# Block-sparse attention scores: four heads at a time in row tiles, with the chunk mask added by 32-row matmuls

## The chip, the cores and the metric

The kernel runs on one core of a Trainium2 chip. The metric is device microseconds for one execution. The kernel before takes 304.92 us (median of three runs, 304.57 to 305.27). Engines are named as in the profile: PE is TensorE (matmuls), PEld its weight loads, DVE VectorE, ACT ScalarE, POOL GpSimd, SP SyncE.

## What is computed

Attention in which each query looks at six chunks of 32 keys, followed by a gated feed-forward layer. Batch 4, 8 heads, 768 positions, head width 64; the feed-forward is 512 to 1536 to 512 on 3072 tokens. The reference, cut:

```python
chunk, top_k, scale = 32, 6, 1 / sqrt(64)
k_min, k_max = k_chunks.min(axis=3), k_chunks.max(axis=3)
ub = sum(maximum(q * k_min, q * k_max), axis=-1)        # a bound for each query and chunk
ub = where(causal, ub, -1e9)
top_chunks = argsort(ub)[..., -top_k:]
scores = scale * (q @ k.T)
mask = (key's chunk is in top_chunks) & (query >= key)
attn = softmax(where(mask, scores, -1e9))
x = (attn @ v)  ->  [3072, 512]
out = (sigmoid(x @ w_gate) * (x @ w_val)) @ w_out
```

## The kernel before

**Order.** The kernel is written as operations with the buffers that they read and write, the engines that may do each, an estimated cost and a rank. `Plan` walks them in estimated time and fixes for every engine one order and for every buffer one slot; the chip then runs each engine's instructions in that order, with semaphores where one engine reads what another wrote. The slots are few: eight PSUM banks (`ps`), of which at most 4 for the feed-forward (`ff`), 3 for scores (`sc`), 2 for attention output (`pv`), 3 for transposes (`pr`), 2 for the bounds (`ub`); 4 buffers `att` for exponentials.

**Tiling.** The 24 blocks of 128 queries are split into eight units of three blocks. Unit 0 holds the first blocks of three batches, which see only their own keys (`first`, scores at L661). Units 1 to 7 go through four stages. `prepare` turns keys and queries (`keys_wide`, `queries_wide` for units 1 and 2, `keys_blocks`, `turn_queries`, `queries_blocks` for the rest) and calls `choose`, which computes the bounds (L811), the sixth largest of each query (L834), and the marks of what is not chosen, turned so that a chunk is a partition (`apt`, L845). `attend` makes scores, exponentials and output; `finish` divides by the sum and turns the result into `xT`; `ffn` does the gate, value and output products (L955, L977). The rank puts `attend` of unit i beside `ffn` of unit i-1, so TensorE has both to do.

**Scores.** The two halves of the heads, `e` and `o`, use 64 partitions each of the turned tensors: head h is pair p = h mod 4, half e = h div 4. A score matmul has 128 rows. Half of them are the 64 components of a head; the other half are the mask. For that, `hk` (keys) holds in its other 64 partitions a fixed pattern `epat`, with -60000 where a partition's chunk is the key's chunk, and `hq` (queries) holds there the marks from `apt`. One matmul thus gives score plus mask. The price is that every head half has an `hk` and an `hq` of its own, filled by copies of 64 partitions (`hk0_`, `hk1_`, `hq0_`, `hq1_`, and `hqm` for the marks), which ACT, DVE or POOL does at L383, L385, L387.

`pack` cuts what a unit's queries see into pieces (key block, first query block, number of query blocks) and lays them into banks of 512 columns. Over units 1 to 7 there are 55 pieces for each head in 23 banks. `attend` goes head by head and bank by bank: one operation `sc` of two to four matmuls into one PSUM bank (L872), one exponential of the bank on ACT (L883), a causal cut of the first bank on POOL (L889), and a head later the output matmuls `pv` (L905). After two heads comes `finish`.

The score matmul:

```python
nc.tensor.matmul(at(t)[:, o:o + 128 * m], hk[b % 2][e_][:, p, 128 * jb:128 * jb + 128],
                 hq[u.side][e_][:, p, 128 * x:128 * (x + m)], start=True, stop=True)
```

Of the kernel before, what the change touches and what calls it, by code (L numbers as in the profile page):

```python
# [15 lines left out]
NEG = -60000.0  # L16
# [322 lines left out]
def kernel(  # L339
# [28 lines left out]
        {"ps": 8, "big": 2, "v": 6, "np": 7, "qf": 2, "qm": 1, "kx": 2, "kt": 3, "ubn": 1, "mx": 1, "apt": 1,  # L368
         "att": 4, "rz": 2, "x": 3, "xt": 2, "gate": 4, "hg": 18, "osb": 2},
        {("ps", "ff"): 4, ("ps", "sc"): 3, ("ps", "pv"): 2, ("ps", "pr"): 3, ("ps", "ub"): 2},  # L370
# [24 lines left out]
    hk = [[lone(f"hk{'eo'[e]}{i}", [128, NP, S]) for e in range(2)] for i in range(2)]  # L395
    hq = [[lone(f"hq{'eo'[e]}{i}", [128, NP, T]) for e in range(2)] for i in range(2)]
# [6 lines left out]
    MASK = [slice(64, 128), slice(0, 64)]  # L403
# [85 lines left out]
    epat = Buf("att", "epat", [64, 2, NC, CH], F16)  # L489
    const("ident", {POOL: (560, 600)}, lambda e: make_identity(nc, ident32), writes=["ident32"], prio=-20)  # L490
    const("epat0", {DVE: (480, 560)}, lambda e: nc.vector.memset(at(epat), 0.0), writes=[epat], prio=-3)

    def pattern(e):
        for i in range(2):
            t = at(epat)[32 * i:32 * i + 32, i]
            nc.gpsimd.affine_select(out=t, in_=t, compare_op=ALU.not_equal, fill=NEG, base=0,
                                    pattern=[[-1, NC], [0, CH]], channel_multiplier=1)

    const("epat", {POOL: (2000, 2040)}, pattern, reads=[epat], writes=[epat], prio=-2.4)
# [3 lines left out]
    for e_ in range(2):  # L503
        const(f"hq{e_}", {DVE: (150, 160)}, lambda e, e_=e_: nc.vector.memset(hq[1][e_][MASK[e_], :, 0:64], 0.0),
              writes=[("hqm", 1, e_, p, "zero") for p in range(NP)])
    for i in range(2):
        const(f"ap{i}", {DVE: (400, 410)}, lambda e, i=i: nc.vector.memset(ap[i], 0.0),
              writes=[("ap", i, 0), ("ap", i, 1)], prio=-0.5 + i)
        const(f"v1{i}", {POOL: (260, 300)}, lambda e, i=i: nc.gpsimd.memset(v16[i][:, :, :, D:D + 1], 1.0),
              writes=[("v16", i, jb) for jb in range(NBLK)], prio=-9 + 6 * i)  # L510
        for e_ in range(2):
            for o in range(2):
                const(f"hkp{i}{e_}{o}", {DVE: dve(2 * S, 4, 64), POOL: pool(2 * S), ACT: act(2 * S, False, 64)},
                      lambda e, i=i, e_=e_, o=o: copy(e, hk[i][e_][MASK[e_], o::2], at(epat)[:, o].rearrange(
                          "p c s -> p (c s)").unsqueeze(1).to_broadcast([64, NP // 2, S])),
                      reads=[epat], writes=[("hkp", i, e_, p) for p in range(o, NP, 2)], prio=0.3 + 0.2 * i, port=True)
# [97 lines left out]
    def first(u, b, x, raw, base):  # L614
# [3 lines left out]
        half = {}  # L618
        for n in "kq":
            t = ps(f"{n}fT_{b}", "pr", [128, NP, 128])  # L620

            def turn(e, t=t, n=n):
                for p in range(NP):
# [3 lines left out]
            half[n] = Buf("np", f"{n}f16_{b}", [128, NP, 128], F16)  # L627
            plan.add(f"{n}f16_{b}", {ACT: act(512), DVE: dve(512)}, lambda e, t=t, h=half[n]: copy(e, at(h), at(t)),
                     reads=[t], writes=[half[n]], prio=next_())
            if n == "k" and b == 0:  # L630
# [8 lines left out]
                for e_ in range(2):  # L639
                    plan.add(f"hkf{e_}", {POOL: pool(512), DVE: dve(512, 4, 64), ACT: act(512, False, 64)},  # L640
                             lambda e, e_=e_: copy(e, hk[0][e_][ROWS[e_], :, 0:128], at(half["k"])[ROWS[e_]]),
                             reads=[half["k"]], writes=[("hk", 0, 0, e_, p) for p in range(NP)], port=True, prio=kn())
# [15 lines left out]
        def scores(e):  # L658
            for p in range(NP):
                for e_ in range(2):  # L660
                    nc.tensor.matmul(at(sc[e_])[:, p], at(half["k"])[ROWS[e_], p], at(half["q"])[ROWS[e_], p], start=True, stop=True)  # L661

        op = plan.add(f"scf_{b}", pe(8 * 56), scores, reads=[half["k"], half["q"]], writes=sc, prio=next_())
# [51 lines left out]
    def keys_wide(u, next_):  # L715
# [5 lines left out]
        for p in range(NP):  # L721
            t = turned(u, 0, p, next_)
            extremes(b % 2, u.name, p, lambda t=t: at(t).rearrange("p (c s) -> p c s", s=CH), u.t, [t], kx,
                     chunks, blocks, False, next_)
            kt = Buf("kt", f"kt_{u.name}_{p}", [128, u.t], F16)
            plan.add(f"kt_{u.name}_{p}", {ACT: act(u.t), DVE: dve(u.t)}, lambda e, t=t, kt=kt: copy(e, at(kt), at(t)),
                     reads=[t], writes=[kt], prio=next_())
            for e_ in range(2):
                plan.add(f"hk{e_}_{u.name}_{p}", {DVE: dve(u.t, 4, 64), POOL: pool(u.t), ACT: act(u.t, False, 64)},
                         lambda e, kt=kt, p=p, e_=e_: copy(e, hk[b % 2][e_][ROWS[e_], p, rows], at(kt)[ROWS[e_]]),  # L730
                         reads=[kt], writes=[("hk", b % 2, jb, e_, p) for jb in blocks], port=True, prio=next_() + 0.3)
        ranges(b % 2, u.name, kx, chunks, blocks, next_)

    def queries_wide(u, next_):
# [3 lines left out]
        for p in range(NP):  # L738
# [6 lines left out]
            for e_ in range(2):  # L745
                plan.add(f"hq{e_}_{u.name}_{p}", {ACT: act(u.t, False, 64), DVE: dve(u.t, 2, 64), POOL: pool(u.t)},
                         lambda e, p=p, e_=e_: copy(e, hq[u.side][e_][ROWS[e_], p, 0:u.t], at(u.qf)[ROWS[e_], p, 0:u.t]),
                         reads=[(u.qf, p)], writes=[("hq", u.side, e_, p)], port=True, prio=next_() + 0.3)


    def keys_blocks(b, raw, next_):
# [4 lines left out]
        for p in range(NP):  # L756
            extremes(par, f"{b}", p, lambda p=p: at(raw)[:, p], S, every, kx, slice(0, NC), blocks, True, next_)
            k16 = Buf("np", f"k16_{b}_{p}", [128, NC, CH], F16)
            kt = Buf("np", f"kt_{b}_{p}", [128, S], F16)
            plan.add(f"k16_{b}_{p}", {POOL: pool(S), DVE: dve(S, 2), ACT: act(S, False)},  # L760
                     lambda e, p=p, k16=k16: copy(e, at(k16), at(raw)[:, p]), reads=every, writes=[k16], prio=next_())
            plan.add(f"kt_{b}_{p}", {DVE: dve(S)}, lambda e, k16=k16, kt=kt: nc.vector.transpose(  # L762
                at(kt), at(k16).rearrange("p c d -> p (c d)")), reads=[k16], writes=[kt], prio=next_())
            for e_ in range(2):
                plan.add(f"hk{e_}_{b}_{p}", {POOL: pool(S), DVE: dve(S, 4, 64), ACT: act(S, False, 64)},
                         lambda e, p=p, e_=e_, kt=kt: copy(e, hk[par][e_][ROWS[e_], p], at(kt)[ROWS[e_]]),
                         reads=[kt], writes=[("hk", par, jb, e_, p) for jb in blocks], port=True, prio=next_())
# [14 lines left out]
    def queries_blocks(u, next_):  # L782
# [5 lines left out]
        for p in range(0, NP, 2):  # L788
# [3 lines left out]
            for e_ in range(2):  # L792
                plan.add(f"hq{e_}_{u.name}_{p}", {DVE: dve(2 * T, 2, 64), ACT: act(2 * T, False, 64), POOL: pool(2 * T)},
                         lambda e, p=p, e_=e_: copy(e, hq[u.side][e_][ROWS[e_], p:p + 2], at(u.qf)[ROWS[e_], p:p + 2]),
                         reads=turned_(p), writes=[("hq", u.side, e_, p + i) for i in range(2)],
                         port=True, prio=next_() + 0.1)


    def choose(u, next_):
# [6 lines left out]
        def bounds(e):  # L806
            for par, lo, hi, _ in spans:
                for m, src in enumerate((u.qf, u.qm)):
                    for p in range(NP):
                        for e_ in range(2):  # L810
                            nc.tensor.matmul(at(ub[e_])[32 * p:32 * p + 32, lo - u.s0:hi - u.s0], kcr[par][ROWS[e_], p, m, :],  # L811
# [31 lines left out]
        apt = Buf("apt", f"apt_{u.name}", [128, 2, u.n], F16)  # L843
        for e_ in range(2):
# [3 lines left out]
            for p in range(0, NP, 2):  # L848
                plan.add(f"hqm{e_}_{u.name}_{p}", {POOL: pool(2 * u.n), DVE: dve(2 * u.n, 4, 64), ACT: act(2 * u.n, False, 64)},
                         lambda e, p=p, e_=e_: copy(  # L850
                             e, hq[u.side][e_][MASK[e_], p:p + 2, u.s0:u.t],
                             at(apt)[32 * p:32 * p + 64, e_, :].unsqueeze(1).to_broadcast([64, 2, u.n])),
                         reads=[(apt, e_)], writes=[("hqm", u.side, e_, p + i) for i in range(2)], port=True, prio=next_())


    def attend(u, base):
        nb = len(u.banks)
        next_ = rank(base, 1.0, H * (3 * nb + 4) + 12)
        late = []
        for h in range(H):  # L860
            pr, last = h // 2, h % 2
            p, e_ = h % NP, h // NP
            att = Buf("att", f"att_{u.name}_{h}", [128, 1920], F16)
            b0 = 0
            for y in range(nb):
                n = 128 * sum(w[3] for w in u.banks[y])
                t = ps(f"sc_{u.name}_{h}_{y}", "sc", [128, n])

                def scores(e, t=t, y=y, p=p, e_=e_):
                    o = 0  # L870
                    for b, jb, x, m in u.banks[y]:
                        nc.tensor.matmul(at(t)[:, o:o + 128 * m], hk[b % 2][e_][:, p, 128 * jb:128 * jb + 128],  # L872
                                         hq[u.side][e_][:, p, 128 * x:128 * (x + m)], start=True, stop=True)
                        o += 128 * m

                reads = [("hk", b % 2, jb, e_, p) for b, jb, _, _ in u.banks[y]]
                reads += [("hkp", b % 2, e_, p) for b, _, _, _ in u.banks[y]] + [("hq", u.side, e_, p), ("hqm", u.side, e_, p)]
                if u.s0:
# [238 lines left out]
```

## Time and profile before

| what | value |
|---|---|
| median of three runs | 304.92 us |
| profiled execution, its own time | 305.61 us |
| span of its profile | 303.7 us |
| mean granted TensorE clock | 0.989 (0.66 between 20 and 30 us, 1.00 in the other windows of 10 us) |
| gate and value matmuls (L955) | 768 of 384 columns |
| output projection matmuls (L977) | 288 of 512 columns |
| score matmuls (L872) | 440, in 184 operations |
| attention output matmuls (L905) | 640 of 65 columns |
| exponentials of scores on ACT (L883) | 184, 90.3 us busy |
| causal cuts on POOL (L889) | 56, 28.3 us busy |

A group line reads: line, engine, operation, output and inputs by the program's names, shape, count, then busy us and mean ns of one, then the idle time of the engine just before these instructions and what ended it. For a matmul, "64\*128" is the rows and columns of the array that it uses. The end of a matmul is modelled and includes a pipeline tail, so a mean for one is longer than the step from it to the next; steps are read from starts. In a timeline a line merges instructions of one kind; its first two numbers are start and length in us. A line of waits has the total us, the number of times and the longest.

### The profile page before, as it was taken

How to read it: one execution, taken by the hardware profiler on the slowest of the kernel's cores; microseconds unless marked ns; L12 is line 12 of the kernel's file. 1: busy time of each engine (PE TensorE's matmuls, PEld its weight loads, DVE VectorE, ACT ScalarE, POOL GpSimd, SP SyncE). 2: the span in 40 equal slices, each digit the busy share in tenths (PEclk: the TensorE clock that was granted, in tenths of full speed). 3: DMA queues.
4: the chain of work that ended last, by engine and by line, in shares of the span. 5: the costliest groups of instructions: out<-in, count | busy, mean ns of one | idle time of the engine just before them, and what ended most of it. 6: DMA issues, size and time to landing. Idle time of an engine off the chain costs nothing.

```text
span 303.7 us, 6957 instructions
## 1 busy us (share of the span) xinstructions
PE 281.5 (93%) x2656; PEld 177.1 (58%) x2656; DVE 184.5 (61%) x550; ACT 203.9 (67%) x412; POOL 97.2 (32%) x158
## 2 busy tenths in 40 slices
PE   3867998999799899999999989999999999999994
PEld 2644665667456456645677555654776467755651
DVE  7684865977998499995435986855634033322420
ACT  7494685969977785956587998454785478833321
POOL 7681023815481433901022649400111011100000
PEclk9996999999999999999999999999999999999999
DMA  7999999999999959909800456101000100001002
GB/s 159 247 223 203 196 199 263 160 185 162 216 168 134 186 106 211 130 21 158 140 2 2 107 121 152 24 0 71 36 2 3 69 37 0 2 33 73 0 4 102
DMA packets 123233, 32.69 MB, mean 108 GB/s; under 512 B 111424, under 2 KB 120128, under 8 KB 123200
## 3 DMA queue, kind: packets, MB, share of 16 engines
q1 hardware_dynamic: 118448, 27.53, 50.4%
q0 software_dynamic: 4752, 4.72, 9.2%
q8 instruction: 21, 0.34, 0.5%
q14 instruction: 12, 0.10, 0.1%
HBM read 30.67 MB, written 6.29 MB: 122 GB/s over the span
## 4 chain that ended last, share of the span: by engine, by line
PE 63%; DMA 14%; DVE 11%; POOL 3%; ACT 3%; issue 2%; SPq 2%; DVEq 0%; ACTq 0%
PE o_u L977 17%; PE g_u L955 15%; PE v_u L955 15%; DMA wo<-in_moe_w_out_dram 9%; PE sc_u L872 6%; PE pv_u L905 4%; DMA vf<-in_v_dram 3%; DVE kt L762 2%; DMA k<-in_k_dram 2%; DVE kx L596 2%; PE ube_u L811 2%; DVE kcr L596 2%; SPq L551 1%; ACT att_u L883 1%; PE xps_u L932 1%
## 5 line engine op out<-in xcount | busy, mean ns | idle before, releaser
L967 DVE SCALAR_TENSOR_TENSOR hg_u<-gate_u,v_u 128x384 f16<-128x384 f16 x96 | 51.9, 547 | 81.2 <-PE v_u L955 65.1
L883 ACT ACTIVATE att_u<-sc_u 128x512 f16<-128x512 f32 (+2 forms) x184 | 90.3, 556 | 5.0 <-PE sc_u L872 4.4
L955 PE MATMUL g_u<-xT_u,wg 128*128 128x384 f16 x384 | 79.2, 329 | 1.5 <-DMA wg<-in_moe_w_gate_dram 1.5
L955 PE MATMUL v_u<-xT_u,wv 128*128 128x384 f16 x384 | 78.8, 328 | 2.0 <-DMA wv<-in_moe_w_val_dram 1.9
L963 ACT ACTIVATE gate_u<-g_u 128x384 f16<-128x384 f32 x96 | 47.2, 492 | 33.2 <-PE g_u L955 18.8
L889 POOL TENSOR_SCALAR_AFFINE_SELECT att_u<-att_u 128x384 f16<-128x384 f16 (+1 forms) x56 | 28.3, 506 | 125.3 <-ACT att_u L883 125.2
L977 PE MATMUL o_u<-wo,hg_u 128*128 128x512 f16 x288 | 66.2, 379 | 1.2 <-DMA wo<-in_moe_w_out_dram 0.9
L955 PEld LDWEIGHTS <-wg 128*128 128x128 f16 x384 | 35.8, 98 | 23.6 <-issue 1.9
L955 PEld LDWEIGHTS <-wv 128*128 128x128 f16 x384 | 36.2, 98 | 22.3 <-DMA wv<-in_moe_w_val_dram 2.3
L977 PEld LDWEIGHTS <-hg_u 128*128 128x128 f16 x288 | 27.4, 98 | 31.9 <-issue 2.2
L986 ACT ACTIVATE osb_u<-o_u 128x512 f32<-128x512 f32 x24 | 14.3, 596 | 34.0 <-PE o_u L977 28.5
L905 PE MATMUL pv_u<-v,att_u 128*128 128x65 f16 x640 | 29.8, 194 | 2.1 <-ACT att_u L883 2.0
L905 PEld LDWEIGHTS <-att_u 128*128 128x128 f16 x640 | 26.5, 98 | 8.9 <-ACT att_u L883 3.7
L872 PE MATMUL sc_u<-hqo,hko 128*128 128x128 f16 (+2 forms) x220 | 28.4, 243 | 2.4 <-ACT att_u L883 2.2
L872 PE MATMUL sc_u<-hqe,hke 128*128 128x128 f16 (+2 forms) x220 | 25.6, 243 | 0.0
L872 PEld LDWEIGHTS <-hko 128*128 128x128 f16 x220 | 16.5, 98 | 7.5 <-issue 3.4
L872 PEld LDWEIGHTS <-hke 128*128 128x128 f16 x220 | 16.3, 98 | 5.5
L588 POOL CAST v<-v 128x512 f16<-128x512 f32 x23 | 14.7, 654 | 8.7 <-DMA v<-in_v_dram 8.6
L924 DVE TENSOR_TENSOR x_u<-pv_u,rz_u 128x384 f16<-128x384 f32 (+1 forms) x28 | 14.8, 530 | 0.6
L383 ACT COPY xT_u<-xps_u 128x384 f16<-128x384 f16 (+1 forms) x19 | 9.1, 476 | 7.9 <-PE xps_u L932 7.5
L612 POOL TENSOR_SCALAR qm_u<-qf_u 128x768 f32<-128x768 f32 (+2 forms) x7 | 12.1, 1729 | 1.9 <-issue 1.8
L834 DVE MAX8 mx_u<-ubn_u 128x8 f32<-128x8 f32 (+16 forms) x152 | 12.3, 158 | 0.1
(118 smaller groups left out, 311.5 us busy)
## 6 DMA issues: line engine op xcount, KB each, us to landing
out_dram<-osb_u SPq DMA_DIRECT2D x24, 256.0 KB, 2.3
v<-in_v_dram SPq DMA_DIRECT2D x23, 256.0 KB, 4.9
k<-in_k_dram SPq DMA_DIRECT2D x12, 384.0 KB, 7.7
q<-in_q_dram SPq DMA_DIRECT2D x12, 384.0 KB, 5.3
wg<-in_moe_w_gate_dram POOLq DMA_DIRECT2D x3, 512.0 KB, 11.3
wv<-in_moe_w_val_dram POOLq DMA_DIRECT2D x3, 512.0 KB, 13.9
wo<-in_moe_w_out_dram POOLq DMA_DIRECT2D x3, 512.0 KB, 24.4
kf<-in_k_dram SPq DMA_DIRECT2D x8, 128.0 KB, 3.6
```

The costliest lines, as they stand in the source:

```text
L588: plan.add(f"v16_{b}_{ib}", {POOL: pool(H * D)}, lambda e: nc.gpsimd.tensor_copy(v16[b % 2][:, ib, :, 0:D], at(t)), reads=[t], writes=[("v ...
L834: nc.vector.max(at(mx)[:, e_, j, :], at(ubn)[:, e_, j, 0:max(8, u.seen[j])])
L872: nc.tensor.matmul(at(t)[:, o:o + 128 * m], hk[b % 2][e_][:, p, 128 * jb:128 * jb + 128], hq[u.side][e_][:, p, 128 * x:128 * (x + m)], sta ...
L883: plan.add(f"exp_{u.name}_{h}_{y}", {ACT: act(n)}, lambda e, t=t, att=att, b0=b0, n=n: nc.scalar.activation(at(att)[:, b0:b0 + n], at(t), ...
L889: nc.gpsimd.affine_select(out=dv, in_=dv, compare_op=ALU.is_ge, fill=0.0, base=0, pattern=[[0, u.m], [1, 128]], channel_multiplier=-1)
L905: nc.tensor.matmul(at(pv)[:, last, x, :], at(att)[:, c:c + 128], v16[b % 2][:, jb, h, :], start=(jb == 0), stop=(jb == ib))
L924: plan.add(f"x_{u.name}_{p}", {DVE: dve(u.t)}, lambda e: nc.vector.tensor_tensor(at(x_).rearrange("p a (e d) -> p e a d", e=2), at(pv)[:, ...
L955: nc.tensor.matmul(at(t), w16[:, c, 128 * fb:128 * fb + 128], at(u.xt)[:, c, :], start=(c == 0), stop=(c == 3))
L963: plan.add(f"tanh_{u.name}_{fb}", {ACT: act(T)}, lambda e, g=g, gate=gate: nc.scalar.activation(at(gate), at(g), AF.Tanh, scale=0.5), read ...
L967: plan.add(f"hg_{u.name}_{fb}", {DVE: dve(T)}, lambda e, w_=w_, gate=gate, hg=hg: nc.vector.scalar_tensor_tensor(at(hg), at(gate), 1.0, at ...
L977: nc.tensor.matmul(at(o), at(hgs[fc])[:, 128 * tb:128 * tb + 128], wo16[:, fc, :], start=(fc == 0), stop=(fc == NFB - 1))
L986: nc.scalar.activation(at(osb), at(o), AF.Copy, scale=0.5) if e == ACT
```

## The change

The head halves no longer have keys and queries of their own. `hk` and `hq` hold both halves, 64 partitions each, and are written once. The pattern `epat` becomes a tensor of four equal groups of 32 partitions. Scores of four heads (two pairs p, both halves) are one operation: for each piece four matmuls of 64 rows into four PSUM banks, then four of 32 rows that add the mask from `apt` and `epat`. So that the four marks of a quad lie in four different groups of 32 partitions, the bounds are written in an order given by `GROUP`. `sc` may hold four banks, `att` has 8 buffers, `apt` 2. `attend` goes by two quads in place of eight heads, and the output matmuls of four heads follow together.

```diff
-        {("ps", "ff"): 4, ("ps", "sc"): 3, ("ps", "pv"): 2, ("ps", "pr"): 3, ("ps", "ub"): 2},
+        {("ps", "ff"): 4, ("ps", "sc"): 4, ("ps", "pv"): 2, ("ps", "pr"): 3, ("ps", "ub"): 2},
...
-    hk = [[lone(f"hk{'eo'[e]}{i}", [128, NP, S]) for e in range(2)] for i in range(2)]
-    hq = [[lone(f"hq{'eo'[e]}{i}", [128, NP, T]) for e in range(2)] for i in range(2)]
+    hk = [lone(f"hk{i}", [128, NP, S]) for i in range(2)]
+    hq = [lone(f"hq{i}", [128, NP, T]) for i in range(2)]
+    epat = lone("epat", [128, NC, CH])
...
-    MASK = [slice(64, 128), slice(0, 64)]
+    GROUP = [[2, 1, 3, 0], [0, 3, 1, 2]]
...
-                const(f"hkp{i}{e_}{o}", {DVE: dve(2 * S, 4, 64), POOL: pool(2 * S), ACT: act(2 * S, False, 64)},
...
+    for g in range(1, 4):
+        const(f"epat{g}", {DVE: dve(S, 4, 64), ACT: act(S, False, 64)}, lambda e, g=g: copy(e, epat[32 * g:32 * g + 32], epat[0:32]),
+              reads=["epat"], writes=[("epat", g)], prio=0.4)
...
-            for e_ in range(2):
-                plan.add(f"hk{e_}_{u.name}_{p}", {DVE: dve(u.t, 4, 64), POOL: pool(u.t), ACT: act(u.t, False, 64)},
...
+            plan.add(f"hk_{u.name}_{p}", {ACT: act(u.t), DVE: dve(u.t)}, lambda e, t=t, p=p: copy(
+                e, hk[b % 2][:, p, rows], at(t)), reads=[t], writes=[("hk", b % 2, jb, p) for jb in blocks], prio=next_() + 0.3)
...
-            plan.add(f"kt_{b}_{p}", {DVE: dve(S)}, lambda e, k16=k16, kt=kt: nc.vector.transpose(
-                at(kt), at(k16).rearrange("p c d -> p (c d)")), reads=[k16], writes=[kt], prio=next_())
-            for e_ in range(2):
-                plan.add(f"hk{e_}_{b}_{p}", {POOL: pool(S), DVE: dve(S, 4, 64), ACT: act(S, False, 64)},
...
+            plan.add(f"hk_{b}_{p}", {DVE: dve(S)}, lambda e, p=p, k16=k16: nc.vector.transpose(
+                hk[par][:, p], at(k16).rearrange("p c d -> p (c d)")), reads=[k16],
+                writes=[("hk", par, jb, p) for jb in blocks], prio=next_())
...
-            for e_ in range(2):
-                plan.add(f"hq{e_}_{u.name}_{p}", {DVE: dve(2 * T, 2, 64), ACT: act(2 * T, False, 64), POOL: pool(2 * T)},
...
+            plan.add(f"hq_{u.name}_{p}", {DVE: dve(2 * u.t, 2), ACT: act(2 * u.t, False), POOL: pool(2 * u.t)},
...
-                            nc.tensor.matmul(at(ub[e_])[32 * p:32 * p + 32, lo - u.s0:hi - u.s0], kcr[par][ROWS[e_], p, m, :],
+                            nc.tensor.matmul(at(ub[e_])[32 * GROUP[e_][p]:32 * GROUP[e_][p] + 32, lo - u.s0:hi - u.s0], kcr[par][ROWS[e_], p, m, :],
...
-            for p in range(0, NP, 2):
-                plan.add(f"hqm{e_}_{u.name}_{p}", {POOL: pool(2 * u.n), DVE: dve(2 * u.n, 4, 64), ACT: act(2 * u.n, False, 64)},
...
-        for h in range(H):
+        for p0 in range(0, NP, 2):
+            quad = [(p, e_) for p in (p0, p0 + 1) for e_ in range(2)]
...
+                sc = {w: ps(f"sc_{u.name}_{w[0]}{w[1]}_{y}", "sc", [128, n]) for w in quad}
...
+                        for p, e_ in quad:
+                            nc.tensor.matmul(at(sc[p, e_])[:, o:o + 128 * m], hk[b % 2][ROWS[e_], p, keys],
+                                             hq[u.side][ROWS[e_], p, lo:hi], start=True, stop=False)
+                        for p, e_ in quad:
+                            g = 32 * GROUP[e_][p]
+                            nc.tensor.matmul(at(sc[p, e_])[:, o + skip:o + 128 * m],
+                                             epat[g:g + 32].rearrange("c a s -> c (a s)")[:, keys],
+                                             at(u.apt)[g:g + 32, e_, lo + skip - u.s0:hi - u.s0], start=False, stop=True)
...
+                reads += [("hq", u.side, p) for p in (p0, p0 + 1)] + [(u.apt, 0), (u.apt, 1), "epat"] + [("epat", g) for g in range(1, 4)]
+                op = plan.add(f"sc_{u.name}_{p0}_{y}", pe(sum(3 * 128 * w[3] / 2.4 + 30 for w in u.banks[y])), scores,
+                              reads=dict.fromkeys(reads), writes=list(sc.values()), prio=next_())
```

`skip` is 64 in the pieces of units 1 and 3 that begin with the first 64 queries of a second block, which see fewer than seven chunks and get no mask.

## The prediction

> **What bounds the kernel now.** I read the page's engine shares first, then its chain of waits, then the windows of ten microseconds, then the groups by shape, and last the timeline around single changes of matmul shape. The shares and the chain:
>
> ```profile
> PE 281.5 (93%) x2656; PEld 177.1 (58%) x2656; DVE 184.5 (61%) x550; ACT 203.9 (67%) x412; POOL 97.2 (32%) x158
> PE 63%; DMA 14%; DVE 11%; POOL 3%; ACT 3%; issue 2%; SPq 2%; DVEq 0%; ACTq 0%
> PE o_u L977 17%; PE g_u L955 15%; PE v_u L955 15%; DMA wo<-in_moe_w_out_dram 9%; PE sc_u L872 6%; PE pv_u L905 4%; DMA vf<-in_v_dram 3%; DVE kt L762 2%; DMA k<-in_k_dram 2%; DVE kx L596 2%; PE ube_u L811 2%; DVE kcr L596 2%; SPq L551 1%; ACT att_u L883 1%; PE xps_u L932 1%
> ```
>
> TensorE sets the end. The 93% alone does not prove it (the ends of matmuls are modelled), so I also took the start stamp of each matmul and subtracted what the one before needs to stream: what is left over sums to 28.5 us in the whole span, 15.5 us of it before 30 us, 9.3 us between 40 and 110 us, and only 3.5 us after 110 us. From 110 us on, a nanosecond added to TensorE is a nanosecond added to the end; 76% of the score work hangs on units 3 to 7, nearly all of it behind that point (84 of 110 piece-quads, counted from `pack`). Before that, part of an addition can fall into gaps.
>
> The scores as they stand, by shape (instructions, then busy us and mean ns of one):
>
> ```profile
> L872 PE MATMUL sc_u<-hqo,hko 128*128 128x128 f16 x148 | 17.3, 219 | 0.4 <-ACT att_u L883 0.4
> L872 PE MATMUL sc_u<-hqe,hke 128*128 128x128 f16 x148 | 16.6, 219 | 0.0
> L872 PE MATMUL sc_u<-hqo,hko 128*128 128x256 f16 x44 | 9.9, 272 | 2.0 <-ACT att_u L883 1.8 <-DVE xT_u L385 0.2
> L872 PE MATMUL sc_u<-hqe,hke 128*128 128x256 f16 x44 | 9.4, 273 | 0.0
> L872 PE MATMUL sc_u<-hqo,hko 128*128 128x384 f16 x28 | 8.8, 326 | 0.0
> L872 PE MATMUL sc_u<-hqe,hke 128*128 128x384 f16 x28 | 8.6, 326 | 0.0
> ```
>
> The reader is to take the counts from here, not the means, which hold a pipeline tail. Start to start in a run of equal matmuls it is 56 ns at 128 columns, 109 at 256, 162 at 384. So the scores cost 296 x 56 + 88 x 109 + 56 x 162 = 35.2 us.
>
> **Part 1, what the packing saves.** Per head there are 37 pieces of 128 queries, 11 of 256 and 7 of 384 (the counts above by 8). Two quads of heads make 74, 22 and 14 piece-quads, 110 in all. Each now takes four matmuls of 64 rows and four of 32. If a pair of 64-row matmuls on different halves runs in the time of one, and four 32-row ones do too, that is 3 streams in place of 4. That pairs run together is shown: the eight 64-row matmuls of L661 at 67.37 us start 4 ns and 52 ns apart in turn, 56 ns for a pair. That eight small tiles run together is shown by L811, whose starts are 6 to 7 ns apart. After: 3 x (74 x 56 + 22 x 109 + 14 x 162) = 26.4 us, less 0.2 us for the 64 columns that units 1 and 3 skip. Saving: 9.0 us.
>
> *A page beside it.* "TensorE: Matmul & The Clock Gate", Part 3 of the Trainium skill, gives four 32-row tiles at 512 columns a measured speed-up of 3.07, not 4. By that figure the mask stream would be 8.8 x 4 / 3.07 = 11.5 us and the total 2.7 us later, an estimate; no row here has 32-row tiles to test it.
>
> **Part 2, what changing the tiling costs.** The scores of before use the same 128-row array as everything around them. The new ones go 128 rows to 64, to 32, back to 64 for the next piece, and at the end back to 128. The trace shows this price where L661 and L811 stand among 128-row matmuls:
>
> ```profile
> 33.34 0.81 PE L955 MATMUL v_u<-xT_u,wv 128*128 128x384 f16 x4
> 34.09 0.45 PE L811 MATMUL ube_u<-qf_u,kcr 64*32 64x320 f32 x1
> ...
> 67.11 0.33 PE L955 MATMUL g_u<-xT_u,wg 128*128 128x384 f16 x1
> 67.37 0.40 PE L661 MATMUL scf<-qf,kf 64*128 64x128 f16 x8
> 67.70 0.39 PE L872 MATMUL sc_u<-hqe,hke 128*128 128x128 f16 x3
> 67.93 0.33 PE L955 MATMUL v_u<-xT_u,wv 128*128 128x384 f16 x1
> ...
> 82.10 0.81 PE L955 MATMUL g_u<-xT_u,wg 128*128 128x384 f16 x4
> 82.75 0.81 PE L955 MATMUL v_u<-xT_u,wv 128*128 128x384 f16 x4
> ```
>
> Four matmuls of 384 columns take 0.65 us to the next start (82.10 to 82.75). At 33.34 it is 0.75 us when the next is a 64-row tile: 0.10 us lost. From 67.11 to 67.37 is 0.26 in place of 0.16, and from 67.37 to 67.70 is 0.33 for four pairs that need 0.22. By the single stamps the gap into L811 is 94 ns in all seven units, after three different lengths (256 against 162, 203 against 109, 149 against 55), and 93 ns out of L661 at 67.5 us. In these rows the weight load too is issued only with its matmul, not 0.1 us ahead as elsewhere, and the first step after the change is 65 ns where 56 is usual. A change of element type at 128 rows costs nothing (955 to the 32-bit transposes of 710: 162 ns), so it is the tiling that is paid for. I take 94 + 10 = 104 ns for a change.
>
> How many: each score operation is one entry and one exit; there are 23 banks per head, so 46 operations: 92 changes. Inside them are 110 changes from 64 to 32 and 110 - 46 = 64 back: 174. In all 266 x 0.104 = 27.7 us. The 92 are priced by rows of the same kind (128 to 64 and back). The 174 between 64 and 32 no row shows. Their bounds: 0 (both are row tilings, and 64-row to 64-row costs nothing) and 0.14 us (L811 back to 128 rows lost about that at 35.36 us). I take 0.104: a price that was the same into 64 rows, out of them and into 64*32 tiles looks like a fixed wait for the array to empty, not like something that grows with the rows.
>
> *A page beside it.* "TensorEngine Tiling (Array Packing)", Key Properties, says that changing the tiling mode, as against the tile, drains the engine, and lists 64 and 32 rows as different modes; it gives no time. With that rule the sum below stands; if 64 and 32 were one mode it would be rival A. The page speaks against this change, and the rows agree as far as 128 against 64 goes.
>
> TensorE: +27.7 - 9.0 = +18.7 us.
>
> **Part 3, the copies that go.** The groups of L383, L385 and L387 that write `hk` and `hq` sum to ACT 31.4, DVE 20.1, POOL 17.6 us. `hk` keeps only the transpose or cast that made `kt`; `hq` keeps half of its casts (one of 128 partitions for two of 64, at the same length); the copies of the turned selection, `epat` into `hk` and half the pattern fill go. Less 25.4 us on ACT, 17.0 on DVE, 15.7 on POOL. No DMA is added, dropped or moved. After 110 us this buys nothing: TensorE is what is waited for there. Between 40 and 110 us it can: around 74 to 82 us ACT is full, with three rows like the first below, while scores wait for its exponentials:
>
> ```profile
> 77.56 0.83 ACT L383 COPY hko<-kt 64x768 f16<-64x768 f16 x1
> ```
>
> ```profile
> PE sc_u L872 <- ACT att_u L883: 2.2, 3, 1.1
> PE pv_u L905 <- ACT att_u L883: 2.0, 5, 1.0
> ```
>
> Of the 9.3 us of gaps there plus 2.2 us between 170 and 180 I take 4 us as recovered (the two waits shown, 4.2 us, are those that freed ACT time would shorten). Bounds: 0, if those gaps move to the next late thing, the key reductions on DVE (L596, L762, solid from 72 to 82 us and not touched); and 11.5, all of them. The selection is a little later for the first heads, since the masks of both halves are read at once, about 2.4 us of DVE (L822 to L845 for the second half), but the four copies behind it are gone; I set that at nothing.
>
> **Part 4, the new wait.** A score operation needs four PSUM banks at once, and all four are emptied by ACT in turn (0.6 us each in the group of L883, 0.5 when back to back). Before, one bank of three was needed. Behind a waiting score matmul stand, in TensorE's order, the gate, value and output products; they have four banks left with `pv`, `pr`, `ub`. The bound below is 0, since ACT is busy about 60% after 110 us and the order puts products between; above, one 0.6 us wait for each of 46 operations is 28 us. Nearest rows: `sc` waited for ACT three times of 184, up to 1.1 us. I take three such half-microsecond waits, 1.5 us, and keep 13 us for rival C.
>
> **Sum.** +18.7 - 4 + 1.5 = +16.2 us. The profiled execution took 305.61 us (span 303.7, 1.9 around it), so 321.8; the median 304.92 is 0.7 below it: 321.1. Forecast **321 us**. Own range 314 to 328 (changes between 64 and 32 at 0.07 to 0.14, recovery 0 to 8).
>
> **Rivals.** A, the other side: 64 and 32 rows change places for free. Then 92 x 0.104 = 9.6 against 9.0 saved, less 4 recovered: -3.4, **301.5 us**. For it: steps within row tiles cost nothing at L661. Against it: every change of tile height in the trace was paid. It decides below (9.0 + 4 - 9.6) / 174 = 20 ns a change. B, part price, about 50 ns: 9.6 + 174 x 0.05 = 18.3 - 9.0 - 2.5 = +6.8, **312 us**. C, the four banks: half of the 28 us bound, 14 in place of 1.5: **334 us**; for it, ACT full from 70 to 80 us; against it, products enough to stand between. D, that the change does not do what it says: four 32-row matmuls run one after another, mask stream 35.2 in place of 8.8: **347 us**; L811's starts speak against it.
>
> **Numbers.** Forecast 0.64, A 0.18, B 0.09, C 0.07, D 0.02. The range reaches 304 (half of A inside) to 330, which leaves out about 0.19. This kernel's runs can tell 0.2%, 0.6 us, from no change. Faster 0.14, within 0.2% 0.04, slower 0.82, from A with its spread of 3 us and the rest.
>
> **What would show it.** In the timeline of after, a score operation of one 128-column piece should read 4 starts in pairs 56 apart, then about 0.15 us to the first 32-row start, then four starts within 20 ns, then 0.15 us to the next: 0.38 us in all against 0.22 for four heads before. If 32-row starts follow 64-row ones after 56 ns, A holds. If starts of one mask group are 56 apart, D. If long idle stands before `sc` with ACT as releaser, C. Gaps of TensorE between 70 and 90 us should shrink. I am wrong if the sum over TensorE's steps does not grow by some 15 to 20 us.

## The result and the profile after

The changed kernel takes **321.65 us** (median of four runs, 320.98 to 323.93) against 305.10 us for the kernel before: a ratio of 1.0557, 95% interval 1.0502 to 1.0613, so 16.5 us slower. The forecast was 321 us. The profiled execution took 320.98 us with a span of 319.3 us (303.7 before).

The page of the changed kernel, engine shares and chain of waits:

```profile
PE 299.3 (94%) x3096; PEld 167.9 (53%) x3096; DVE 170.3 (53%) x512; ACT 180.0 (56%) x380; POOL 75.3 (24%) x132
PE 86%; DMA 4%; DVE 4%; ACT 2%; POOL 1%; issue 1%; SPq 0%; DVEq 0%; ACTq 0%
PE v_u L941 20%; PE g_u L941 20%; PE o_u L963 17%; PE sc_u L849 9%; PE sc_u L853 6%; PE pv_u L892 6%; DMA wv<-in_moe_w_val_dram 3%; PE ube_u L790 2%; PE xps_u L918 1%; DVE kcr L585 1%; DVE hk L746 1%; DVE kx L585 1%; DMA qf<-in_q_dram 1%; PE qfT L613 1%; PE qT_u L701 1%
```

The other engines did get lighter (ACT 204 to 180 us, VectorE 184 to 170, GpSimd 97 to 75), but that is not where the time is decided: the chain is now 86% TensorE where it was 63%, and the scores' share of it went from 6% to 15% (L849 and L853). The line numbers moved: L872 became L849 (keys) and L853 (masks), L883 became L865, L955 became L941.

The group lines of the scores, by shape:

```profile
L849 PE MATMUL sc_u<-hq,hk 64*128 64x128 f16 x296 | 21.1, 221 | 0.0
L853 PE MATMUL sc_u<-apt_u,epat 32*128 32x128 f16 x280 | 16.4, 225 | 0.0
L849 PE MATMUL sc_u<-hq,hk 64*128 64x256 f16 x88 | 8.6, 274 | 0.0
L849 PE MATMUL sc_u<-hq,hk 64*128 64x384 f16 x56 | 7.0, 328 | 0.0
```

The busy sums of these groups look hardly larger than before (they merge what overlaps and hold pipeline tails). They don't show the loss. It is seen only between the starts, in the timeline of one score operation of three 128-column pieces (first number start in us, then length):

```profile
239.71 0.28 PE L918 MATMUL xps_u<-ident,x_u 128*128 128x128 f16 x2
239.92 0.29 PE L849 MATMUL sc_u<-hq,hk 64*128 64x128 f16 x4
240.13 0.23 PE L853 MATMUL sc_u<-apt_u,epat 32*128 32x128 f16 x4
240.30 0.28 PE L849 MATMUL sc_u<-hq,hk 64*128 64x128 f16 x4
240.52 0.23 PE L853 MATMUL sc_u<-apt_u,epat 32*128 32x128 f16 x4
240.69 0.29 PE L849 MATMUL sc_u<-hq,hk 64*128 64x128 f16 x4
240.91 0.23 PE L853 MATMUL sc_u<-apt_u,epat 32*128 32x128 f16 x4
241.07 0.50 PE L941 MATMUL g_u<-xT_u,wg 128*128 128x384 f16 x2
```

From the first key group to the next is 0.38 us (239.92 to 240.30); the same work of four heads was four steps of 56 ns, 0.22 us. Nothing idles in the profile's sense and no releaser is named: the idle column is empty, because the modelled end of each matmul reaches past the next start. By single stamps, the two key pairs are 64 ns apart, the first mask starts 148 to 149 ns after the last key matmul (55 of it streaming), the four masks start 3 to 4 ns apart, and the next key pair 156 ns after the last of them.

Where the time went, by an account of TensorE's steps: from start to start, each step is split into what the matmul streams, up to about 0.1 us where the tiling changes, and the rest, gaps. From the first to the last matmul:

| us | before | after |
|---|---|---|
| score streams | 35.2 | 28.9 |
| changes of tiling (22, 284) | 2.3 | 27.6 |
| all other streams | 229.6 | 229.6 |
| gaps | 28.0 | 24.5 |
| sum | 295.1 | 310.6 |

So TensorE's work grew by 19.0 us (-6.3 and +25.3), and gaps gave back 3.5: 15.5 us between these two executions, as their spans say too (15.6). The medians are 16.5 us apart.

### The profile page after: what moved, and what is told of

The parts are those of the page before. It is cut to its first block, busy times and chain, and to the rows that moved or that the text cites. A ratio compares the mean times of both kernels' runs of the same rounds, so it can differ in the third digit from the quotient of the medians.

```text
span 319.3 us, 7733 instructions
## 1 busy us (share of the span) xinstructions
PE 299.3 (94%) x3096; PEld 167.9 (53%) x3096; DVE 170.3 (53%) x512; ACT 180.0 (56%) x380; POOL 75.3 (24%) x132
## 4 chain that ended last, share of the span: by engine, by line
PE 86%; DMA 4%; DVE 4%; ACT 2%; POOL 1%; issue 1%; SPq 0%; DVEq 0%; ACTq 0%
PE v_u L941 20%; PE g_u L941 20%; PE o_u L963 17%; PE sc_u L849 9%; PE sc_u L853 6%; PE pv_u L892 6%; DMA wv<-in_moe_w_val_dram 3%; PE ube_u L790 2%; PE xps_u L918 1%; DVE kcr L585 1%; DVE hk L746 1%; DVE kx L585 1%; DMA qf<-in_q_dram 1%; PE qfT L613 1%; PE qT_u L701 1%
## 5 line engine op out<-in xcount | busy, mean ns | idle before, releaser
L865 ACT ACTIVATE att_u<-sc_u 128x512 f16<-128x512 f32 (+3 forms) x184 | 86.4, 549 | 45.4 <-PE sc_u L853 45.4
L941 PE MATMUL g_u<-xT_u,wg 128*128 128x384 f16 x384 | 79.7, 330 | 1.7 <-ACT qn_u L383 1.0
L941 PE MATMUL v_u<-xT_u,wv 128*128 128x384 f16 x384 | 78.9, 328 | 1.8 <-DMA wv<-in_moe_w_val_dram 1.8
L963 PE MATMUL o_u<-wo,hg_u 128*128 128x512 f16 x288 | 67.8, 383 | 0.0
L872 POOL TENSOR_SCALAR_AFFINE_SELECT att_u<-att_u 128x384 f16<-128x384 f16 (+1 forms) x56 | 27.5, 511 | 120.3 <-ACT att_u L865 119.9
L941 PEld LDWEIGHTS <-wv 128*128 128x128 f16 x384 | 35.9, 98 | 26.9 <-issue 2.4
L941 PEld LDWEIGHTS <-wg 128*128 128x128 f16 x384 | 36.0, 99 | 24.6 <-issue 1.5
L849 PE MATMUL sc_u<-hq,hk 64*128 64x128 f16 (+2 forms) x440 | 36.7, 245 | 0.0
L853 PE MATMUL sc_u<-apt_u,epat 32*128 32x128 f16 (+4 forms) x440 | 28.3, 247 | 0.0
L892 PE MATMUL pv_u<-v,att_u 128*128 128x65 f16 x640 | 25.1, 195 | 0.9 <-ACT att_u L865 0.8
L892 PEld LDWEIGHTS <-att_u 128*128 128x128 f16 x640 | 23.2, 99 | 4.4 <-ACT att_u L865 1.1
L849 PEld LDWEIGHTS <-hk 64*128 64x128 f16 x440 | 12.5, 94 | 18.9 <-issue 13.8
L853 PEld LDWEIGHTS <-epat 32*128 32x128 f16 x440 | 11.1, 91 | 16.8 <-issue 9.1
L908 DVE RECIPROCAL rz_u<-pv_u 128x6 f32<-128x6 f32 (+1 forms) x28 | 5.0, 186 | 16.9 <-PE pv_u L892 16.7
L585 DVE TRANSPOSE_TENSOR_REDUCE kcr<-k 128x24 f32<-128x768 f32 x12 | 11.4, 949 | 1.5 <-DMA k<-in_k_dram 1.5
```

Source lines behind the costliest of these rows:

```text
L585: plan.add(f"kx{m}_{name}_{p}", {DVE: dve(size)}, lambda e, m=m, op=op: nc.vector.tensor_reduce(out=outs[m](), in_=src(), op=op, axis=AX.X ...
L849: nc.tensor.matmul(at(sc[p, e_])[:, o:o + 128 * m], hk[b % 2][ROWS[e_], p, keys], hq[u.side][ROWS[e_], p, lo:hi], start=True, stop=False)
L853: nc.tensor.matmul(at(sc[p, e_])[:, o + skip:o + 128 * m], epat[g:g + 32].rearrange("c a s -> c (a s)")[:, keys], at(u.apt)[g:g + 32, e_, ...
L865: plan.add(f"exp_{u.name}_{w[0]}{w[1]}_{y}", {ACT: act(n)}, lambda e, t=sc[w], att=att[w], b0=b0, n=n: nc.scalar.activation(at(att)[:, b0: ...
L872: nc.gpsimd.affine_select(out=dv, in_=dv, compare_op=ALU.is_ge, fill=0.0, base=0, pattern=[[0, u.m], [1, 128]], channel_multiplier=-1)
L892: nc.tensor.matmul(at(pv)[:, i, x, :], at(a)[:, c:c + 128], v16[b % 2][:, jb, h, :], start=(jb == 0), stop=(jb == ib))
```

## The experiments

### Quads and banks without row tiles

The changed kernel with its whole order, but one 128-row matmul over both halves per head:

```diff
-                            nc.tensor.matmul(at(sc[p, e_])[:, o:o + 128 * m], hk[b % 2][ROWS[e_], p, keys],
-                                             hq[u.side][ROWS[e_], p, lo:hi], start=True, stop=False)
-                        for p, e_ in quad:
-                            g = 32 * GROUP[e_][p]
...
+                            nc.tensor.matmul(at(sc[p, e_])[:, o:o + 128 * m], hk[b % 2][:, p, keys],
+                                             hq[u.side][:, p, lo:hi], start=True, stop=True)
```

> The changed kernel with its order, quads, banks and copies, but each score matmul is one of 128 rows over both halves, so that no tiling changes; the sums of two heads are scored and the chunk mask is left out. Theory (a change of tiling costs 0.104 us, 266 of them less the few at the bounds, here 262 go): 321.65 - 27.2 + 8.8 of longer streams = 303 us, and steps of 56, 109 and 162 ns at the scores. Rival (four banks at once, and four heads in one operation, cost the time): still above 315 us.

Measured 304.58 us, ratio to the kernel before 0.996 (0.9936 to 0.9984). Its timeline has the score operations in plain steps of 56 ns:

```profile
228.94 0.33 PE L913 MATMUL xps_u<-ident,x_u 128*128 128x128 f16 x3
229.11 0.83 PE L849 MATMUL sc_u<-hq,hk 128*128 128x128 f16 x12
```

Twelve starts within 0.61 us (0.83 less the 0.22 tail of the last) are 11 steps of 56 ns, and the entry from 228.94 is three steps, 0.17: no loss. Everything else of the change (four heads at once, four banks, fewer copies) is in this kernel, and it is not slower than before. The row tiles alone carry the loss: 321.65 - 304.58 = 17.1 us. The rival of the four banks falls.

### Masks in 64-row tiles

Two forms. In the first the bounds are laid out by quad, so that a head's marks lie in the half of its keys, and the pattern has two variants with 32 rows of zeros:

```diff
+                                             epat[ROWS[e_], p % 2].rearrange("c a s -> c (a s)")[:, keys],
+                                             at(u.apt)[ROWS[e_], p // 2, lo + skip - u.s0:hi - u.s0], start=False, stop=True)
...
-                            nc.tensor.matmul(at(ub[e_])[32 * GROUP[e_][p]:32 * GROUP[e_][p] + 32, lo - u.s0:hi - u.s0], kcr[par][ROWS[e_], p, m, :],
+                            nc.tensor.matmul(at(ub[p // 2])[64 * e_ + 32 * (p % 2):64 * e_ + 32 * (p % 2) + 32, lo - u.s0:hi - u.s0], kcr[par][ROWS[e_], p, m, :],
```

> The mask by 64-row matmuls, 32 rows of whose pattern are zero, on the half that the head's keys use; what is computed stays the same. The 174 changes between 64 and 32 rows go, 92 remain, and the mask stream doubles. Theory: 321.65 - 174 x 0.104 + 8.6 = 312 us; a score operation of one 128-column piece has starts 56 apart throughout. Rival (only the way into row tiles and out costs, 64 against 32 is free): 321.65 + 8.6 = 330 us. Rival of the four banks: 321 us or more.

Measured 317.49 us (ratio 1.0391, 1.0354 to 1.0427): 4.2 us faster than the changed kernel, where 9.6 was expected. The steps say why. The score part came out as planned (110 changes in the kernel in place of 284), but the bounds (L790) took 16.8 us of TensorE against 9.1; of these 7.7 us about 5 show in the time, by the next run. In the timeline of this kernel:

```profile
106.30 0.74 PE L790 MATMUL ube_u<-qf_u,kcr 64*32 64x320 f32 x8
106.86 0.72 PE L790 MATMUL ubo_u<-qf_u,kcr 64*32 64x320 f32 x8
```

`ube` and `ubo` now run one after the other, 0.56 us apart. In the changed kernel their starts alternate 6 to 7 ns apart. By quad, pairs p and p + 2 of a half use the same rows and the same 32 columns of the array, so eight matmuls share four tiles; by half, they use eight different tiles. A shared bank does not explain it: by the stamps, four matmuls into the bank of `ube` start 6 to 7 ns apart, while those into the other bank come 0.56 us later. That was a side effect of this edit, so it was taken out: bounds as in the changed kernel, and a pattern of zeros in place of `epat`, so that the chunk mask is left out while every matmul is issued.

```diff
+    zpat = lone("zpat", [128, NC, CH])
...
+                                             zpat[ROWS[e_]].rearrange("c a s -> c (a s)")[:, keys],
+                                             at(u.apt)[ROWS[e_], e_, lo + skip - u.s0:hi - u.s0], start=False, stop=True)
```

> The mask by 64-row matmuls as in the run mask64, but with the bounds placed as in the changed kernel and a pattern of zeros, so that the chunk mask is left out and every matmul is still issued. Theory: the 7.8 us that the bounds cost more in mask64 go, 92 changes remain, scores take 35.2 + 92 x 0.104 = 44.8 us of TensorE: 311 us. Rival (mask64's miss of 5 us came from the 64-row masks themselves): 317 us.

Measured 312.45 us (ratio 1.0223, 1.0178 to 1.0267), 1.5 us from the expectation and 4.6 from the rival. Its timeline around a score operation:

```profile
233.16 0.33 PE L919 MATMUL xps_u<-ident,x_u 128*128 128x128 f16 x3
233.42 0.29 PE L851 MATMUL sc_u<-hq,hk 64*128 64x128 f16 x4
233.55 0.28 PE L854 MATMUL sc_u<-apt_u,zpat 64*128 64x128 f16 x4
233.66 0.28 PE L851 MATMUL sc_u<-hq,hk 64*128 64x128 f16 x4
...
233.99 0.28 PE L854 MATMUL sc_u<-apt_u,zpat 64*128 64x128 f16 x4
234.20 0.82 PE L942 MATMUL g_u<-xT_u,wg 128*128 128x384 f16 x4
```

Inside, keys and masks follow at 0.11 us, two pairs of 56 ns; only the first group (0.13) and the two ends (0.26 in place of 0.17, 0.21 in place of 0.11) pay. Twice the mask stream, and still 9.2 us faster than with 32-row masks: a change between 64 and 32 rows costs like one between 128 and 64. Rival A of the prediction, that it is free, falls here. So does another reading, that a mask waits because it adds into the bank that a key matmul has just written: here it does the same, at the full pace of 56 ns for a pair.

### Masks left out, masks twice

Without the mask matmuls the chunk mask is left out. Twice means the same group of four again, right behind the first.

```diff
-                        for p, e_ in quad:
-                            g = 32 * GROUP[e_][p]
-                            nc.tensor.matmul(at(sc[p, e_])[:, o + skip:o + 128 * m],
...
```

> The changed kernel without the mask matmuls: the chunk mask is left out. 92 changes and half the key stream of before. Theory: the masks cost 174 changes and 8.6 us of streams, 26.7 us; 295 us, up to 298 if TensorE now waits for exponentials. Rival (only entering and leaving row tiles costs): 321.65 - 8.6 = 313 us.

Measured 297.01 us (ratio 0.9721, 0.9677 to 0.9765): the masks cost 24.6 us, not the 8.6 of the rival. TensorE's work fell by 27.8 us (10.7 of streams, 17.1 of changes), so some 3 us of it did not reach the end. Most of that can be seen between 121 and 125 us, where the four matmuls of a piece, in two operations, start one by one, 0.35 to 0.49 us apart, while ACT's exponentials of the banks follow each other at 0.37 to 0.49 us:

```profile
122.15 0.32 PE L849 MATMUL sc_u<-hq,hk 64*128 64x384 f16 x1 [0.17 <-ACT att_u L860]
122.64 0.32 PE L849 MATMUL sc_u<-hq,hk 64*128 64x384 f16 x1 [0.17 <-ACT att_u L860]
```

That is the new wait of Part 4 of the prediction, in a kernel whose TensorE has less to do.

> Each group of four 32-row mask matmuls is issued twice, one after the other; the mask is then -120000 in place of -60000. 110 more groups, no change of tiling more. Theory: the streams alone, 8.6 us: 330 us, starts of the second group 56, 109 or 162 ns after the first. Rival (each group of four pays anew): 330 + 110 x 0.104 = 342 us. Rival (four do not run together): 321.65 + 35 = 356 us.

Measured 330.70 us (ratio 1.082, 1.0761 to 1.0879), 9.1 us more than once. The timeline:

```profile
239.82 0.23 PE L853 MATMUL sc_u<-apt_u,epat 32*128 32x128 f16 x4
239.88 0.23 PE L858 MATMUL sc_u<-apt_u,epat 32*128 32x128 f16 x4
240.04 0.29 PE L849 MATMUL sc_u<-hq,hk 64*128 64x128 f16 x4
```

The second group starts 0.06 us after the first (by the stamps 56 to 57 ns from the last mask of the one to the first of the other, 109 to 110 at 256 columns, 163 at 384): four matmuls in the time of one, no price. So the 32-row stream is as cheap as hoped, and rival D falls. What costs is getting there.

### Twice the changes

Two heads' keys, their masks, then the other two:

```diff
+                        for pair in (quad[:2], quad[2:]):
+                            for p, e_ in pair:
...
```

> Each piece in two goes: two heads' keys, their masks, the other two heads' keys, their masks. Twice the changes inside a piece: 220 more, and a second mask stream of 8.6 us. Theory: 321.65 + 220 x 0.104 + 8.6 = 353 us. Rival (the price belongs to the operation, not to each change): 330 us.

Measured 352.30 us (ratio 1.1555, 1.1493 to 1.1618).

```profile
250.54 0.23 PE L850 MATMUL sc_u<-hq,hk 64*128 64x128 f16 x2
250.70 0.23 PE L854 MATMUL sc_u<-apt_u,epat 32*128 32x128 f16 x2
250.86 0.23 PE L850 MATMUL sc_u<-hq,hk 64*128 64x128 f16 x2
```

Every group of two now starts 0.16 us after the one before, 56 ns of stream and 104 of change. The price is linear in the number of changes: 88, 262 and 482 changes more than in the kernel before take 8.2, 25.3 and 49.0 us in the runs with keys alone, in the changed kernel and here, 93 to 102 ns each.

### What the copies were worth

The kernel before, head by head, but with `hk` and `hq` kept once for both halves, no pattern, no marks and none of their copies; the score matmul runs over both halves, so the sums of two heads are scored and the mask is left out.

```diff
-    hk = [[lone(f"hk{'eo'[e]}{i}", [128, NP, S]) for e in range(2)] for i in range(2)]
-    hq = [[lone(f"hq{'eo'[e]}{i}", [128, NP, T]) for e in range(2)] for i in range(2)]
+    hk = [[lone(f"hk{i}", [128, NP, S])] * 2 for i in range(2)]
+    hq = [[lone(f"hq{i}", [128, NP, T])] * 2 for i in range(2)]
...
-            for p in range(0, NP, 2):
-                plan.add(f"hqm{e_}_{u.name}_{p}", {POOL: pool(2 * u.n), DVE: dve(2 * u.n, 4, 64), ACT: act(2 * u.n, False, 64)},
```

> The kernel before with its heads one by one and its 128-row score matmuls, but keys and queries are kept once, as in the changed kernel: the copies into half heads, of the pattern and of the marks are gone; the sums of two heads are scored and the chunk mask is left out. TensorE's work is the same. Theory (freed ACT and VectorE time shortens TensorE's gaps between 40 and 110 us and at 170 us): 4 us less, 301 us, at most 11 less. Rival (a bound elsewhere is late next, the twelve key operations of a batch on VectorE): within 1.5 us of the kernel before.

Measured 304.52 us, ratio 0.9979 (0.9949 to 1.0009): no difference that can be told. The theory falls, and the rival's number holds. The waits that had named ACT did shrink: those of `sc` and `pv` for its exponentials from 4.2 to 1.3 us. TensorE's gaps between 40 and 110 us are 8.2 us here against 9.2 before, and the 2.3 us between 170 and 180 are gone. But other gaps came: about 1.5 us at 124 us, where the bounds wait for GpSimd, and about 2 us before 40 us, where the granted clock is 0.55 and 0.94 in the windows from 20 and from 30 us (0.66 and 1.00 before). The waits of TensorE in this kernel (total us, times, longest):

```profile
PE xpsf L672 <- DVE xf L665: 2.9, 3, 1.8
...
PE ube_u L781 <- POOL qm_u L593: 1.3, 1, 1.3
...
PE pv_u L867 <- ACT att_u L845: 0.9, 1, 0.9
```

### The new gap at 130 us

In the changed kernel one stretch has a gap that was not there: 6.1 us between 130 and 150 us, where the kernel before had 0.7. TensorE's wait and, in VectorE's timeline, what stood before the quotient:

```profile
PE xps_u L918 <- DVE x_u L910: 2.1, 2, 1.7
```

```profile
125.53 0.20 DVE L908 RECIPROCAL rz_u<-pv_u 128x6 f32<-128x6 f32 x1 [1.10 <-PE pv_u L892]
125.70 0.98 DVE L585 TRANSPOSE_TENSOR_REDUCE kcr<-k 128x24 f32<-128x768 f32 x1
...
135.20 0.94 DVE L746 STREAM_TRANSPOSE hk<-k 128x768 f16<-128x768 f16 x1
136.06 0.52 DVE L910 TENSOR_TENSOR x_u<-pv_u,rz_u 128x384 f16<-128x384 f32 x1
```

The quotient could run at 125.7, behind its reciprocal; the planned order has the twelve key operations of the next batch between the two, 10.4 us. Only part of the gap is named waiting: the granted clock fell to 0.86 there, and matmuls right after it run slow (512 columns at steps of 0.43 us at 139 us, where 0.22 is usual):

```profile
130.00:140.00 10.00, 7.04 (x66) 3.63 (x64) 9.90 (x21) 5.00 (x12) 2.63 (x3) 0.86 1.03 204
```

(Columns: window, its length, busy us of PE, PEld, VectorE, ACT, GpSimd with counts, granted clock, DMA share, GB/s.) Two runs tried to take this gap out. The first gives the planner the measured cost of a score operation:

```diff
-                op = plan.add(f"sc_{u.name}_{p0}_{y}", pe(sum(3 * 128 * w[3] / 2.4 + 30 for w in u.banks[y])), scores,
+                op = plan.add(f"sc_{u.name}_{p0}_{y}", pe(94 + sum(3 * 128 * w[3] / 2.4 + 220 for w in u.banks[y])), scores,
```

> Only the cost that the order is planned with is changed: 94 ns for a score operation and 220 in place of 30 ns for a piece. Theory: TensorE's work stays as it is; the wait of 5.3 us between 130 and 145 us, where the quotient of the attention output stands on VectorE behind twelve key operations, is the order's doing and goes: 316 us. Rival (the wait comes from the keys' DMA or from VectorE's load): within 1 us of 321.6.

Measured 321.47 us (ratio 1.0531, 1.0488 to 1.0573): a miss; the rival's number came, but not for its reason. The gap between 130 and 150 us did go (0.6 us left), and one of 5.4 us appeared between 90 and 110 us, where the bounds now stand behind the twelve operations of another batch:

```profile
PE ube_u L790 <- DVE qf_u L759: 4.0, 1, 4.0
```

The second, in the kernel before, ranks the reciprocal and the quotient ahead:

```diff
+        first_, next_ = next_, lambda: first_() - 1.0
         rz = Buf("rz", f"rz_{u.name}_{p}", [128, 2, u.m])
```

> The kernel before, with the reciprocal and the quotient of the attention output (L922, L924) ranked ahead by one unit, so that they are planned before the twelve key operations of a batch on VectorE. Theory (the gaps of 2 to 5 us belong to whatever stands behind those twelve operations, and freeing one sets the next late): within 1 us of the kernel before. Rival (the quotient alone is what is late): the 2.3 us of gaps between 170 and 180 us go, 303 us.

Measured 309.06 us (ratio 1.0128, 1.0097 to 1.0159), slower than either expected. The gap between 170 and 180 us stayed (2.6 us). Between 100 and 110 us, where TensorE runs out of products and goes at the pace of the exponentials, the gaps grew from 2.5 to 4.1 us, and 1.2 us came between 240 and 250 us. Over the whole run TensorE's waits of `pv` for exponentials went from 2.0 us (5 times) to:

```profile
PE pv_u L905 <- ACT att_u L883: 3.3, 10, 1.1
```

TensorE's gaps grew by about 3 us in all, of the 3.7 that the medians are apart. Part of the theory stands (the next thing becomes late), but it did not name this one, and neither run is a gain. Which order would be free of such gaps stays open.

### Eight kernels in one account

Scores and changes on TensorE from the trace of each run (changes beyond the 22 that the kernel before has), and what is left of the measured time. In keys_only the 2.2 us by which six score matmuls waited for their banks are left out of the streams:

| run | score streams | changes | time | rest |
|---|---|---|---|---|
| kernel before | 35.2 | 0 | 305.1 | 269.9 |
| no_copies | 35.2 | 0 | 304.5 | 269.3 |
| rows128 | 35.2 | 0 | 304.6 | 269.4 |
| keys_only | 18.2 | 8.2 | 297.0 | 270.6 |
| mask64_zero | 35.6 | 8.2 | 312.5 | 268.7 |
| changed kernel | 28.9 | 25.3 | 321.65 | 267.5 |
| mask_twice | 38.5 | 24.1 | 330.7 | 268.1 |
| split | 36.4 | 49.0 | 352.3 | 266.9 |

The rest is 266.9 to 270.6 us while the sum of the other two goes from 26.4 to 85.4. Of 59.0 us that the scores take more on TensorE, 55.3 show in the time; part of the difference is the wait for banks seen with keys alone. Three runs are not in the table: true_cost has the scores and the time of the changed kernel; mask64 leaves 266.2 once the 7.7 us of its bounds are taken out too; finish_first leaves 273.9, more than any in the table: it changes the order and not the scores.

## Why the prediction was right

**Part 1, the saving.** Priced at 26.2 us of score streams and 2.7 of slower first steps (266 times 10 ns); measured 28.9. Pairs of 64-row and fours of 32-row tiles do run in the time of one matmul. The Trainium skill's 3.07 for four row tiles ("TensorE: Matmul & The Clock Gate", Part 3) would have made it 2.7 us more; in this stream a group of four cost 56 ns at 128 columns, 109 at 256 and 163 at 384, the step of a single matmul, so up to 384 columns it is four here, and the measurement decides. No piece here has the page's 512 columns.

**Part 2, the changes of tiling.** Priced at 25.0 us besides those first steps (266 x 94 ns); measured 25.3 us for 262 (three score operations are followed directly by the bounds and one follows them, so four changes serve both). The step that no row of before showed, 64 to 32 rows and back, is 93 ns in and 101 ns out, like 128 to 64. That extrapolation from L661 and L811 carried the forecast, and the runs with 64-row masks, with split groups and without masks confirm it. "TensorEngine Tiling (Array Packing)", Key Properties, says that a change of mode drains the engine; the trace shows a loss at every change and adds the size, 0.10 us with the slower first step. Whether it is the array's emptying that takes this time, or the weight load that comes only with its matmul, no run here separates.

**Part 3, the copies.** Wrong. The prediction put 4 us on freed ACT and VectorE time; the run without copies gained 0.6 us, not distinguishable from none. The two waits that it went by did shrink, by 2.9 us together, but gaps elsewhere took their place, which is the lower bound that the prediction had named and not taken. In the changed kernel the gaps between 40 and 110 us did shrink (9.2 to 2.6 us), but also with quads and 128-row tiles (2.5), and the run without copies kept 8.2; so lighter engines alone do not do it; it took the new order, and that order brought the gap at 130 us (6.5 us with 128-row tiles too). The new order with the copies kept was not run.

**Part 4, the four banks.** The 1.5 us of waits for exponentials did not come: no wait of `sc` for ACT is among the waits of after. It did come where TensorE has less to do: about 2 us with keys alone, and about 1 us with 128-row tiles, where at 127.5 us the four matmuls of a 256-column piece start 0.38 to 0.50 us apart. A wait of about that size came elsewhere in the changed kernel, `xps` for the quotient, 2.1 us.

**The sum.** Parts 3 and 4 together were forecast at -2.5 us; the kernel with all of them and no row tiles is 1.2 us faster than the kernel before that was run beside it (0.4%). Parts 1 and 2 were forecast at +18.7 us; TensorE's work did grow by 19.0, but against the kernel with 128-row tiles the time is only 17.1 us longer. These two errors, +1.3 and -1.6, have opposite signs and nearly cancel; that 321 came so close to 321.65 is in part luck.

**The rivals.** A (free between 64 and 32) and D (row tiles in turn) are excluded by steps and by runs, C (the banks, 14 us) by the run with 128-row tiles. B would have needed half the price.

No version that computes the whole beat the kernel before: the three that were as fast or faster (128-row tiles, no copies, keys alone) leave the chunk mask out.

## What to carry to other kernels

Row tiling pays by the column and is paid for by the change. Here two changes per piece, 0.2 us, stood against 56, 109 or 162 ns of stream saved for four heads at once; only pieces of more than about 460 columns (an estimate: 0.2 us at 56 ns for 128; the longest here has 384) would have paid for the way to 32 rows and back. So count how often the tile height changes, not how many rows idle, and group all work of one height.

Freed time on an engine is worth what the next late thing leaves of it: before pricing it, look for what stands behind the named wait, and test the removal alone.

A loss at changes of tiling shows in no idle column and hardly in busy sums. Compare steps from start to start with the same matmul in an unbroken run.

## What the runs showed of the hardware that was not expected

A change of tiling costs almost the same whichever way it goes: 95 ns from 128 to 64 rows, 93 from 64 to 32, 101 from 32 to 64, 101 from 32 to 128 (medians in the changed kernel). Behind a second group of masks the way out is 147 ns in place of 157, so some 10 ns of a group's start show up at its first step, wherever that is. And matmuls of 64 rows that shared rows and columns with each other cost the bounds 16.8 us in place of 9.1, with the same number of matmuls of the same size: a tile's place decides what runs together, as much as its size.
